# Key maxima of an agent-attention kernel: two scans of the scores in PSUM per chunk, one per half of the agents, in the place of one strided pass over the transposed scores

## The chip, the cores and the metric

The kernel runs on one core of a Trainium2 chip. The metric is the device time of one execution in microseconds (us). The time before is 364.25 us, the median of three runs (364.14, 364.25, 367.25).

## What is computed

Four batches of 12608 tokens with 128 channels, and 49 agents per batch. A softmax over all tokens (agents against keys) pools the values into 49 rows; a softmax over the agents (queries against agents) spreads these rows back over the tokens. Then a mixture-of-experts step replaces, per batch, the 128 tokens with the highest gate score.

```python
def sm(a, b):
    s = scale * (a @ b.transpose(0, 2, 1))
    s = s - s.max(-1, keepdims=True)
    e = np.exp(s)
    return e / (e.sum(-1, keepdims=True) + 1e-09)
a2k = sm(agents, k)          # (B, 49, 12608)
agent_v = a2k @ v
q2a = sm(q, agents)
x = q2a @ agent_v
...
top_idx = np.argpartition(-scores[b], capacity)[:capacity]   # scores = x @ w_gate
out[b, top_idx] = x[b, top_idx] + g[:, None] * ye            # ye: two-layer expert
```

The change touches one quantity of this: for each agent, the maximum of its scores over all keys, `s.max(-1)` in `a2k`.

## The kernel before, in words

**Tiling.** A batch's tokens are 99 columns of 128. They are worked in seven chunks (15, 15, 15, 15, 15, 15 and 9 columns). A chunk of keys or queries comes from memory with the channels on the partitions, 960 KB for 15 columns, into one of five input buffers (`inp`, shared with the values).

**Scores (`scores`, L205).** For each chunk, and for each half `h` of the agents (32 each, the 49 agents padded to 64), four matmuls write one PSUM tile `S`: matmul `i` puts 32 agents on partitions 32i to 32i+31, for a quarter of the chunk's tokens (480 columns for a 15-column chunk, 288 for a 9-column one). The four use different partitions of the tile. In a profile each of these fp32 matmuls leaves two records, so a half is 8 records and a chunk 16. VectorE then transposes the tile in blocks of 32x32 into an SBUF tile (`sk` for keys, `sq` for queries) in which tokens are on the partitions (L220). There are two `S` buffers in PSUM (SB = 2), one half each; a half is refilled when the instructions that read it are done.

**Key side.** `k_front` (L228) does the scores of a key chunk and then reduces the transposed tile to the chunk's maximum for each of 49 agents on each partition (L238, `mx`): the input is read as "p t a -> p a t", so that consecutive elements are 64 floats apart. After a batch's seventh chunk `k_max` (L242) takes the maximum over the chunks (L245, `m1`), turns it with a TensorE transpose (L247, `mT`), takes the maximum over the 128 partitions (L250, `m2`), spreads it over all partitions by a diagonal matrix (L252, `dg`) and a matmul with ones (L254, `mB`), and copies it to SBUF (L257, `mb`). `k_exp` (L264, L267) waits for `mb`: GpSimd subtracts it from each chunk, ScalarE takes the exponential. Then the matmuls `av` (L282) pool the values, `v_finish` makes the weights `ws` (L320 to L324).

**Query side.** `q_scores` (L329) does the same transposes, then a maximum over the agents of each token (L340, `qm`, read contiguously); `q_exp`, `q_high` and `q_low` make fp16 pairs `f` on GpSimd and ScalarE; `q_turn` transposes them on TensorE (`fT`, L392) and copies them out (`ft`, L393). `q_gate` (L407, `pg`) gives the gate scores, `topk` finds the 128 largest by 16 rounds of counting (L489 to L500, `jk`, `bk`, `js`), `q_out` (L448, `po`) makes the output tiles `og`, which are stored. `expert` gathers the chosen rows (L633), and scatters the new rows (L686) when the batch's output is stored.

**What sets the order.** The program is written chunk by chunk in the order of `load_order`, with priorities for some steps (RANK, TOPK, CHASE and so on). A scheduler then fixes one static order per engine, by its own model of durations; at run time each engine goes through its list in that order and waits where an operand isn't ready. So another duration or another number of instructions on one engine changes the lists of the others too.

Of the kernel before, what the change touches and what calls it, by code (L numbers as in the profile page):

```python
# [13 lines left out]
F32 = mybir.dt.float32  # L14
# [5 lines left out]
ALU = mybir.AluOpType  # L20
AX = mybir.AxisListType
PSUM = bass.MemoryType.PSUM

P = 128
# [3 lines left out]
A = 49  # L28
AP_ = 64
CHUNKS = [15, 15, 15, 15, 15, 15, 9]  # L30
STARTS = [sum(CHUNKS[:i]) for i in range(len(CHUNKS))]
NCH = len(CHUNKS)
# [93 lines left out]
def agent_attention_moe(ctx, tc, qT, kT, va, agT, wgb, w1, w2, consts, qs, outs, capacity):  # L126
    nc = tc.nc
# [13 lines left out]
    sm = ctx.enter_context(tc.tile_pool(name="sm", bufs=2))  # L141
# [39 lines left out]
    idf = const.tile([P, P], F32, name="idf")  # L181
# [3 lines left out]
    ones_f = const.tile([2 * A, P], F32, name="ones_f")  # L185
# [14 lines left out]
    def load(src, name, w):  # L200
        t = inp.tile([P, TMAX * (C + 1)], F32, tag="in", name=name)
        newest["load"] = nc.sync.dma_start(t[:, :w], src).ins
        return t

    def scores(src, b, c, dst):  # L205
        n = CHUNKS[c]
        w = 32 * n
        col = P * STARTS[c]
        xt = load(src[b, :, col:col + P * n], f"xT_{b}_{c}", P * n)
        for h in range(2):  # L210
            ps = psS.tile([P, 512], F32, tag="S", name=f"S_{b}_{c}_{h}")
            for i in range(4):
                nc.tensor.matmul(  # L213
                    ps[32 * i:32 * i + 32, :w],
                    ag_sb[:, b, 32 * h:32 * h + 32],
                    xt[:, w * i:w * i + w],
                    start=True,
                    stop=True,
                )
            nc.vector.transpose(  # L220
                dst[:, :n, 32 * h:32 * h + 32],
                ps[:, :w].rearrange("p (t c) -> p t c", c=32),
            )

    st = [{} for _ in range(B)]
    tail, begun, turns = set(), [], []
# [2 lines left out]
    def k_front(b, c):  # L229
        n = CHUNKS[c]  # L230
        d = st[b]
        if c == 0:
            d["S"] = {}
            d["mx"] = sm.tile([P, NCH, A], F32, tag="mx", name=f"mx_{b}")
        s = skp.tile([P, TMAX, AP_], F32, tag="sk", name=f"sk_{b}_{c}")
        scores(kT, b, c, s)
        d["S"][c] = s
        nc.vector.tensor_reduce(  # L238
            d["mx"][:, c], s[:, :n, :A].rearrange("p t a -> p a t"), axis=AX.X, op=ALU.max
        )  # L240

    def k_max(b):  # L242
        d = st[b]
        m1 = sm.tile([P, A], F32, tag="m1", name=f"m1_{b}", bufs=1)
        nc.vector.tensor_reduce(m1, d["mx"].rearrange("p c a -> p a c"), axis=AX.X, op=ALU.max)  # L245
        pt = psT.tile([P, 512], F32, tag="T", name=f"mT_{b}")
        nc.tensor.transpose(pt[:A, :P], m1, idf)  # L247
        yield
        m2 = sm.tile([A, 1], F32, tag="m2", name=f"m2_{b}", bufs=1)
        nc.vector.tensor_reduce(m2, pt[:A, :P], axis=AX.X, op=ALU.max)  # L250
        dg = sm.tile([P, A], F32, tag="m1", name=f"dg_{b}", bufs=1)[:A]
        nc.vector.tensor_scalar(dg, idf[:A, :A], m2, None, op0=ALU.mult)  # L252
        pb = psT.tile([P, 512], F32, tag="T", name=f"mB_{b}")
        nc.tensor.matmul(pb[:, :A], ones_f[:A], dg, start=True, stop=True)  # L254
        yield
        mb = sm.tile([P, A], F32, tag="mb", name=f"mb_{b}")
        nc.vector.tensor_copy(mb, pb[:, :A])  # L257
        d["mb"] = mb
        yield
# [72 lines left out]
    def q_scores(b, c):  # L332
        n = CHUNKS[c]
        d = st[b]
        s = qp.tile([P, TMAX, AP_], F32, tag="sq", name=f"sq_{b}_{c}", bufs=3)
        d["q", c] = s
        scores(qT, b, c, s)
        m = sm.tile([P, TMAX], F32, tag="qm", name=f"qm_{b}_{c}", bufs=3)
        d["qm", c] = m
        nc.vector.tensor_reduce(m[:, :n], s[:, :n, :A], axis=AX.X, op=ALU.max)  # L340
# [390 lines left out]
    for i in range(LAST):  # L731
# [15 lines left out]
        for b, c in get("k"):  # L747
            k_front(b, c)
            if c == NCH - 1:
                chains.append((b, k_max(b)))  # L750
# [105 lines left out]
```

## Time and profile before

| | |
|---|---|
| median of three runs | 364.25 us |
| the profiled execution | 367.46 us, of which its span from first to last instruction is 365.2 us |
| VectorE (DVE) busy | 287.6 us, 79% of the span, 761 instructions |
| TensorE (PE) busy | 308.0 us, 84% |
| GpSimd (POOL) busy | 182.9 us, 50% |
| ScalarE (ACT) busy | 169.6 us, 46% |
| chain that ended last | PE 52%, DVE 32%, POOL 5%, issue 4%, DMA 4%, ACT 2% |

The profiled execution lies 3.2 us above the median, near the slowest of the three runs. "Busy" is the time in which at least one instruction of an engine was under way. PEld is TensorE's loading of weights. The chain that ended last is followed back from the last instruction: at each step to what released it. In rows of waits, "A <- B: t, n" means that A's engine stood idle t us in n places until B was done. Lines of instructions are numbered as in the kernel before.

### The profile page before, as it was taken

How to read it: one execution, taken by the hardware profiler on the slowest of the kernel's cores; microseconds unless marked ns; L12 is line 12 of the kernel's file. 1: busy time of each engine (PE TensorE's matmuls, PEld its weight loads, DVE VectorE, ACT ScalarE, POOL GpSimd, SP SyncE). 2: the span in 40 equal slices, each digit the busy share in tenths (PEclk: the TensorE clock that was granted, in tenths of full speed). 3: DMA queues.
4: the chain of work that ended last, by engine and by line, in shares of the span. 5: the costliest groups of instructions: out<-in, count | busy, mean ns of one | idle time of the engine just before them, and what ended most of it. 6: DMA issues, size and time to landing. Idle time of an engine off the chain costs nothing.

```text
span 365.2 us, 9066 instructions
## 1 busy us (share of the span) xinstructions
PE 308.0 (84%) x3669; PEld 199.9 (55%) x3669; DVE 287.6 (79%) x761; ACT 169.6 (46%) x293; POOL 182.9 (50%) x149
## 2 busy tenths in 40 slices
PE   3775885998959999989999778989989999977774
PEld 0111344554435656446545438365479998967763
DVE  1999997669989998987899795176696989797432
ACT  1012455321544644645543156044667649796740
POOL 0046698714693655794415099033322015894532
PEclk9999997899987999999999995898999799996699
DMA  8999989689994999994998995455068875786390
GB/s 298 408 420 415 346 281 391 228 304 334 420 377 132 367 359 336 347 385 141 396 337 308 403 354 178 157 189 222 2 263 293 351 286 209 305 355 257 133 375 16
DMA packets 18586, 106.63 MB, mean 292 GB/s; under 512 B 2544, under 2 KB 3952, under 8 KB 18544
## 3 DMA queue, kind: packets, MB, share of 16 engines
q1 hardware_dynamic: 17472, 105.07, 75.5%
q8 instruction: 29, 0.48, 0.5%
q0 software_dynamic: 256, 0.52, 0.4%
q10 hardware_dynamic: 816, 0.46, 0.4%
q14 instruction: 13, 0.11, 0.1%
HBM read 79.83 MB, written 26.21 MB: 290 GB/s over the span
## 4 chain that ended last, share of the span: by engine, by line
PE 52%; DVE 32%; POOL 5%; issue 4%; DMA 4%; ACT 2%; POOLq 0%; ACTq 0%; DVEq 0%
PE S L213 17%; PE po L448 10%; PE av L282 9%; PE fT L392 6%; DVE mx L238 6%; DVE sk L220 5%; DVE sq L220 3%; PE pg L407 3%; DVE qm L340 2%; PE bk L494 2%; DMA cst<-consts 2%; DVE qm L351 2%; POOL sq L347 2%; DMA out<-og 1%; POOL f L373 1%
## 5 line engine op out<-in xcount | busy, mean ns | idle before, releaser
L213 PE MATMUL S<-xT,ag_sb 128*32 128x480 f32 (+1 forms) x896 | 117.0, 586 | 15.2 <-DMA ag_sb<-agT 6.3
L393 ACT COPY ft<-fT 98x896 f16<-98x896 f16 (+2 forms) x49 | 42.7, 899 | 58.4 <-PE fT L392 58.2
L448 PE MATMUL po<-ws,ft 98*128 98x128 f16 x792 | 63.7, 235 | 5.8 <-DVE ws L323 2.2
L347 POOL TENSOR_TENSOR sq<-sq,qm 128x735 f32<-128x735 f32 (+1 forms) x28 | 38.2, 1369 | 56.6 <-DVE qm L340 52.3
L448 PEld LDWEIGHTS <-ft 98*128 98x128 f16 x792 | 54.8, 107 | 14.2 <-issue 13.4
L282 PE MATMUL av<-v,sk 128*64 128x129 f32 x792 | 60.9, 291 | 0.6 <-ACT sk L267 0.6
L213 PEld LDWEIGHTS S<-xT,ag_sb 128*32 128x32 f32 x896 | 24.9, 113 | 61.5 <-issue 16.8
L282 PEld LDWEIGHTS av<-v,sk 128*64 128x64 f32 x792 | 50.2, 144 | 11.5 <-issue 7.5
L373 POOL TENSOR_TENSOR f<-sq,f 128x735 f16<-128x735 f32 (+1 forms) x28 | 41.2, 1476 | 28.7 <-ACT f L368 23.7
L264 POOL TENSOR_TENSOR sk<-sk,mb 128x735 f32<-128x735 f32 (+1 forms) x28 | 46.7, 1712 | 10.0 <-DVE mb L257 10.0
L220 DVE STREAM_TRANSPOSE sk<-S 128x480 f32<-128x480 f32 (+1 forms) x56 | 35.0, 640 | 12.0 <-PE S L213 11.2
L348 ACT ACTIVATE sq<-sq,lift 128x735 f32<-128x735 f32 (+1 forms) x28 | 24.8, 887 | 41.0 <-POOL sq L347 40.8
L392 PEld LDWEIGHTS <-f 128*98 128x98 f16 x396 | 26.9, 127 | 23.0 <-issue 16.4
L238 DVE TENSOR_REDUCE mx<-sk 128x49 f32<-128x735 f32 (+1 forms) x28 | 38.9, 1390 | 0.3
L392 PE MATMUL fT<-idh,f 128*98 128x128 f16 x396 | 34.1, 227 | 5.4 <-POOL f L373 4.5
L220 DVE STREAM_TRANSPOSE sq<-S 128x480 f32<-128x480 f32 (+1 forms) x56 | 34.7, 636 | 5.0 <-PE S L213 4.7
L368 ACT CAST f<-sq 128x735 f16<-128x735 f32 (+1 forms) x28 | 22.0, 789 | 31.2 <-POOL sq L362 24.5
L362 POOL TENSOR_TENSOR sq<-sq,qm 128x735 f32<-128x735 f32 (+1 forms) x14 | 19.1, 1367 | 31.7 <-DVE qm L355 28.2
L467 POOL TENSOR_TENSOR og<-og,r 128x512 f32<-128x512 f32 (+2 forms) x33 | 30.3, 946 | 7.6 <-ACT og L466 5.0
L496 DVE TENSOR_REDUCE bk<-bk 128x3 f32<-128x99 f32 x64 | 16.5, 259 | 21.1 <-PE bk L494 20.6
L457 ACT ACTIVATE og<-po,iv 128x512 f32<-128x512 f32 (+1 forms) x35 | 22.3, 669 | 20.6 <-PE po L448 13.4
L267 ACT ACTIVATE sk<-sk 128x735 f32<-128x735 f32 (+1 forms) x28 | 22.1, 797 | 18.7 <-POOL sk L264 18.2
(143 smaller groups left out, 380.4 us busy)
## 6 DMA issues: line engine op xcount, KB each, us to landing
v<-va SPq DMA_DIRECT2D x24, 967.5 KB, 6.9
xT<-kT SPq DMA_DIRECT2D x24, 960.0 KB, 7.9
xT<-qT SPq DMA_DIRECT2D x24, 960.0 KB, 8.3
out<-og SPq DMA_DIRECT2D x24, 960.0 KB, 4.3
v<-va SPq DMA_DIRECT2D x4, 580.5 KB, 4.8
xT<-kT SPq DMA_DIRECT2D x4, 576.0 KB, 6.5
xT<-qT SPq DMA_DIRECT2D x4, 576.0 KB, 5.6
out<-og SPq DMA_DIRECT2D x4, 576.0 KB, 5.9
```

What stands on the lines that cost most here:

```text
L213: nc.tensor.matmul(ps[32 * i:32 * i + 32, :w], ag_sb[:, b, 32 * h:32 * h + 32], xt[:, w * i:w * i + w], start=True, stop=True,)
L220: nc.vector.transpose(dst[:, :n, 32 * h:32 * h + 32], ps[:, :w].rearrange("p (t c) -> p t c", c=32),)
L238: nc.vector.tensor_reduce(d["mx"][:, c], s[:, :n, :A].rearrange("p t a -> p a t"), axis=AX.X, op=ALU.max)
L264: nc.gpsimd.tensor_tensor(sv, sv, st[b]["mb"].unsqueeze(1).broadcast_to([P, n, A]), op=ALU.subtract)
L282: nc.tensor.matmul(d["av"][o:o + AP_, :C + 1], d["S"][c][:, t], d["v", c][:, t], start=(j < 2), stop=(j >= COLS - 2),)
L347: nc.gpsimd.tensor_tensor(sv, sv, m[:, :n].unsqueeze(2).broadcast_to([P, n, A]), op=ALU.subtract)
L348: nc.scalar.activation(sv, sv, AF.Exp, scale=SCALE, bias=lift)
L373: nc.gpsimd.tensor_tensor(f[:, :n, A:], st[b]["q", c][:, :n, :A], f[:, :n, :A], op=ALU.subtract)
L392: nc.tensor.transpose(pt[:2 * A, P * t:P * t + P], f[:, t0 + t, :], idh)
L393: (nc.vector.tensor_copy if TURN[b][t0 // 8] == "V" else nc.scalar.copy)(d["ft", c][:2 * A, P * t0:P * (t0 + nt)], pt[:2 * A, :P * nt])
L448: nc.tensor.matmul(p3[:, t], q_tile(b, c, t0 + t), d["W"][:, i, :C], start=(i == 0), stop=(i == 1))
L467: nc.gpsimd.tensor_tensor(o4, o4, rate.broadcast_to([P, nt, C]), op=ALU.mult)
```

## The change

`scores` gets an argument `top`. On the key side, after each of the two transposes of a chunk, a VectorE reduction reads the same PSUM tile, contiguously along the tokens, and writes one maximum per partition (a partition being one agent of the half and one quarter of the tokens). The strided pass over `sk` goes. `mx` shrinks from 49 to 2 values per chunk and partition, and `k_max` works on 2 values per partition: the transpose gives 2 rows of 128, `m2` is the maximum over the four quarters, `dg` spreads it on a 2-row diagonal, and the matmul with ones has 2 rows and 64 columns.

```diff
-    def scores(src, b, c, dst):
+    def scores(src, b, c, dst, top=None):
...
                 ps[:, :w].rearrange("p (t c) -> p t c", c=32),
             )
+            if top is not None:
+                nc.vector.tensor_reduce(top[:, h:h + 1], ps[:, :w], axis=AX.X, op=ALU.max)
...
-            d["mx"] = sm.tile([P, NCH, A], F32, tag="mx", name=f"mx_{b}")
+            d["mx"] = sm.tile([P, NCH, 2], F32, tag="mx", name=f"mx_{b}")
...
-        scores(kT, b, c, s)
+        scores(kT, b, c, s, d["mx"][:, c])
         d["S"][c] = s
-        nc.vector.tensor_reduce(
-            d["mx"][:, c], s[:, :n, :A].rearrange("p t a -> p a t"), axis=AX.X, op=ALU.max
-        )
...
-        m1 = sm.tile([P, A], F32, tag="m1", name=f"m1_{b}", bufs=1)
-        nc.vector.tensor_reduce(m1, d["mx"].rearrange("p c a -> p a c"), axis=AX.X, op=ALU.max)
+        m1 = sm.tile([P, 2], F32, tag="m1", name=f"m1_{b}", bufs=1)
+        nc.vector.tensor_reduce(m1, d["mx"].rearrange("p c h -> p h c"), axis=AX.X, op=ALU.max)
         pt = psT.tile([P, 512], F32, tag="T", name=f"mT_{b}")
-        nc.tensor.transpose(pt[:A, :P], m1, idf)
+        nc.tensor.transpose(pt[:2, :P], m1, idf)
         yield
-        m2 = sm.tile([A, 1], F32, tag="m2", name=f"m2_{b}", bufs=1)
-        nc.vector.tensor_reduce(m2, pt[:A, :P], axis=AX.X, op=ALU.max)
-        dg = sm.tile([P, A], F32, tag="m1", name=f"dg_{b}", bufs=1)[:A]
-        nc.vector.tensor_scalar(dg, idf[:A, :A], m2, None, op0=ALU.mult)
+        m2 = sm.tile([2, 32], F32, tag="m2", name=f"m2_{b}", bufs=1)
+        nc.vector.tensor_reduce(
+            m2, pt[:2, :P].rearrange("h (i a) -> h a i", a=32), axis=AX.X, op=ALU.max
+        )
+        dg = sm.tile([2, 2, 32], F32, tag="dg", name=f"dg_{b}", bufs=1)
+        nc.vector.tensor_tensor(
+            dg, m2.unsqueeze(1).broadcast_to([2, 2, 32]),
+            idf[:2, :2].unsqueeze(2).broadcast_to([2, 2, 32]), op=ALU.mult,
+        )
         pb = psT.tile([P, 512], F32, tag="T", name=f"mB_{b}")
-        nc.tensor.matmul(pb[:, :A], ones_f[:A], dg, start=True, stop=True)
+        nc.tensor.matmul(pb[:, :AP_], ones_f[:2], dg.rearrange("k h a -> k (h a)"), start=True, stop=True)
```

The static order moves with it. Three places follow. In the names, `S_0_6_1` is batch 0, chunk 6, second half (`sk` and `sq` tell keys from queries); the last number is a counter. From L224 on, the changed kernel's lines are shifted by 2, and behind `k_max` by 4.

**VectorE at the end of batch 0's keys**, where `k_max` makes `mb`, before:

```order
L250 TENSOR_REDUCE m2_0_336<-mT_0_314 49x1
L340 TENSOR_REDUCE qm_0_3_357<-sq_0_3_342 128x15
L393 COPY ft_0_0_316<-fT_0_0_0_317 98x1024
L252 TENSOR_SCALAR dg_0_338<-idf_102,m2_0_336 49x49
L220 STREAM_TRANSPOSE sk_1_0_367<-S_1_0_0_370 128x15x32
L220 STREAM_TRANSPOSE sk_1_0_367<-S_1_0_1_376 128x15x32
L257 COPY mb_0_359<-mB_0_340 128x49
L238 TENSOR_REDUCE mx_1_366<-sk_1_0_367 128x49
```

and now:

```order
L249 TENSOR_REDUCE m2_0_343<-mT_0_321 2x32
L397 COPY ft_0_0_323<-fT_0_0_0_324 98x1024
L344 TENSOR_REDUCE qm_0_3_364<-sq_0_3_349 128x15
L253 TENSOR_TENSOR dg_0_345<-m2_0_343,idf_102 2x64
L220 STREAM_TRANSPOSE sk_1_0_374<-S_1_0_0_377 128x15x32
L225 TENSOR_REDUCE mx_1_373<-S_1_0_0_377 128x1
L220 STREAM_TRANSPOSE sk_1_0_374<-S_1_0_1_384 128x15x32
L225 TENSOR_REDUCE mx_1_373<-S_1_0_1_384 128x1
L261 COPY mb_0_366<-mB_0_347 128x49
```

Each transpose is followed by its scan. The copy of `mb_0` stood between the transposes and the pass of the next chunk; now it stands behind both transposes and both scans of it.

**TensorE at the scores of query chunk 3 of batch 3**, between the gate matmuls `pg` of batch 2, before:

```order
L407 MATMUL pg_2_2631<-ws_2_2551,ft_2_5_2478 128x3
L213 MATMUL S_3_3_0_2893<-xT_3_3_2891,ag_sb_94 32x480
L407 LDWEIGHTS ft_2_5_2478
L407 MATMUL pg_2_2631<-ws_2_2551,ft_2_5_2478 128x3
L213 MATMUL S_3_3_0_2893<-xT_3_3_2891,ag_sb_94 32x480
L407 LDWEIGHTS ft_2_5_2478
L407 MATMUL pg_2_2631<-ws_2_2551,ft_2_5_2478 128x3
L213 MATMUL S_3_3_0_2893<-xT_3_3_2891,ag_sb_94 32x480
```

and now:

```order
L411 MATMUL pg_2_2659<-ws_2_2579,ft_2_4_2390 128x3
L213 MATMUL S_3_3_0_2921<-xT_3_3_2919,ag_sb_94 32x480 x4
L213 MATMUL S_3_3_1_2927<-xT_3_3_2919,ag_sb_94 32x480 x3
L411 LDWEIGHTS ft_2_4_2390
L411 MATMUL pg_2_2659<-ws_2_2579,ft_2_4_2390 128x3
L213 MATMUL S_3_3_1_2927<-xT_3_3_2919,ag_sb_94 32x480
```

All eight score matmuls of the chunk stood alone, each between gate matmuls; now seven stand together and one alone. Key chunk 1 of batch 3 stood in the same way, in six pieces among `fT` matmuls; now its two halves are whole.

**TensorE at the scores of query chunk 0 of batch 2**, before:

```order
L213 MATMUL S_2_0_0_1472<-xT_2_0_1470,ag_sb_94 32x480 x4
L213 MATMUL S_2_0_1_1478<-xT_2_0_1470,ag_sb_94 32x480 x4
L448 LDWEIGHTS ft_0_6_730
L448 MATMUL po_0_6_4_2592<-ws_0_904,ft_0_6_730 128x128
L448 LDWEIGHTS ft_0_6_730
```

and now:

```order
L213 MATMUL S_2_0_0_1491<-xT_2_0_1489,ag_sb_94 32x480 x4
L286 MATMUL av_1_1150<-v_1_3_1507,sk_1_3_630 64x129 x15
L213 MATMUL S_2_0_1_1497<-xT_2_0_1489,ag_sb_94 32x480 x3
L498 LDWEIGHTS ones_b_111
L498 MATMUL bk_0_1067<-jk_hi_0_3_1123,ones_b_111 128x99
L498 LDWEIGHTS ones_b_111
L498 MATMUL bk_0_1067<-jk_hi_0_3_1123,ones_b_111 128x99
```

Here a half that was whole is now in two pieces (the fourth matmul follows behind the counting matmuls), and the second half stands behind 15 value matmuls. In the whole of TensorE's list the score halves were cut into pieces 12 more than the 112 halves (10 of 480 columns, 2 of 288); now they are cut into 9 more (6 and 3). SyncE's list, which issues the loads, has not changed.

## Rows read from the trace of the kernel before

**Rows 1.** [...] Under the dots the same view for line L238 alone: busy us of DVE and number of passes.
```profile
8.00:60.00 52.00, 38.13 (x376) 13.39 (x368) 48.68 (x76) 16.27 (x20) 30.89 (x21) 1.00 0.96 374
60.00:205.00 145.00, 132.40 (x1608) 75.68 (x1608) 128.84 (x289) 62.43 (x79) 82.64 (x58) 0.95 0.87 323
205.00:265.00 60.00, 53.34 (x562) 32.16 (x563) 38.18 (x103) 26.79 (x33) 27.76 (x18) 0.89 0.56 202
265.00:365.00 100.00, 82.42 (x1122) 78.13 (x1120) 71.14 (x289) 62.81 (x161) 40.73 (x43) 0.89 0.66 260
...
8.00:60.00 52.00, 14.28 (x10) 1.00 0.96 374
60.00:205.00 145.00, 24.64 (x18) 0.95 0.87 323
```

**Rows 2.** The chain that ended last in order of time: start us, length us, what. The first 40 us.
```profile
10.75 1.42 DVE mx L238
12.17 1.16 DVE sk L220 x2
13.36 1.48 DVE mx L238
14.83 1.16 DVE sk L220 x2
...
32.19 1.48 DVE mx L238
...
35.23 0.86 DVE mx L238
```

**Rows 3.** The waits of all engines from 8 to 60 us, and under the dots from 60 to 205 us: engine and line, for whom it waited, us in total, times, longest.
```profile
PEld S L213 <- DVE sk L220: 15.8, 19, 1.7
...
DVE sk L220 <- PE S L213: 4.7, 9, 0.9
PEld S L213 <- DVE sk L220: 0.8, 2, 0.5
```

**Rows 4.** Groups of instructions by line and shape: line, engine, operation, out<-in, shapes, count, then busy us and mean ns of one, then idle time before them.
```profile
L238 DVE TENSOR_REDUCE mx<-sk 128x49 f32<-128x735 f32 x24 | 35.2, 1468 | 0.2
L238 DVE TENSOR_REDUCE mx<-sk 128x49 f32<-128x441 f32 x4 | 3.7, 919 | 0.1
L340 DVE TENSOR_REDUCE qm<-sq 128x15 f32<-128x735 f32 x24 | 21.6, 902 | 0.2
L340 DVE TENSOR_REDUCE qm<-sq 128x9 f32<-128x441 f32 x4 | 2.4, 598 | 0.0
L220 DVE STREAM_TRANSPOSE sk<-S 128x480 f32<-128x480 f32 x48 | 31.4, 668 | 11.8 <-PE S L213 11.1
L220 DVE STREAM_TRANSPOSE sk<-S 128x288 f32<-128x288 f32 x8 | 3.7, 469 | 0.2 <-PE S L213 0.2
```

**Rows 5.** The same view for the small operations of `k_max`.
```profile
L245 DVE TENSOR_REDUCE m<-mx 128x49 f32<-128x343 f32 x4 | 3.1, 766 | 0.1
L252 DVE TENSOR_SCALAR dg<-idf,m 49x49 f32<-49x49 f32 x4 | 1.7, 434 | 0.0
L250 DVE TENSOR_REDUCE m<-mT 49x1 f32<-49x128 f32 x4 | 1.1, 263 | 0.6 <-PE mT L247 0.5
L257 DVE COPY mb<-mB 128x49 f32<-128x49 f32 x4 | 0.7, 166 | 0.0
```

**Rows 6.** The timeline around 42 us: start, length, engine, line, operation, out<-in, count, and in brackets the idle time before it.
```profile
41.91 0.16 DVE L257 COPY mb<-mB 128x49 f32<-128x49 f32 x1
...
42.15 1.80 POOL L264 TENSOR_TENSOR sk<-sk,mb 128x735 f32<-128x735 f32 x1 [1.37 <-DVE mb L257]
```

**Rows 7.** The chain again, at a whole chunk of scores, then in the two places where the score matmuls stood alone, and at a small one.
```profile
73.85 1.75 PE S L213 x16
...
160.00 0.92 PE S L213 x2
...
231.06 0.92 PE S L213 x2
...
238.32 0.92 PE S L213 x2
...
262.13 0.60 PE S L213 x2
```

**Rows 8.** The chain between 83 and 205 us, where it goes through the key maxima: the first and the last of nine such pieces, and the last of two maxima over the chunks.
```profile
83.59 1.44 DVE mx L238
...
203.87 0.91 DVE mx L238
204.81 0.78 DVE m L245
```

**Rows 9.** The timeline at the end: the gather of batch 2's rows, the transpose of them, and the scatter of its new rows.
```profile
335.19 0.99 POOL L633 DMA_INDIRECT xq<-q,idx  x1 [4.40 <-DVE js_lo L500]
...
345.21 0.42 PE L642 MATMUL qT<-idf,xq 128*128 128x128 f32 x1
...
359.77 1.03 POOL L686 DMA_INDIRECT out<-ye,idx  x1 [8.58 <-DVE ye L679]
```

**Rows 10.** Who let TensorE and its weight loads wait at the tiles `xT` (the loaded keys and queries), over the whole span: releaser, us, times.
```profile
  DVE sk L220: 21.1, 28
...
  DMA ag_sb<-agT: 12.6, 2
```

## The prediction

> **What bounds the kernel now.** I read the stages first (the windows view), because the key maxima lie in a part of the span only: 10 of the 28 strided passes run from 8 to 60 us, 18 from 60 to 205 us, none later [rows 1]. So 160 us of 365 can change only through an earlier start or another order. In the first stage VectorE is busy 48.68 of 52 us and TensorE 38.13; in the second TensorE leads, 132.40 of 145 us, with VectorE close behind at 128.84 [rows 1]. The chain in order of time shows the same for the start: it runs along VectorE, pass, two transposes, pass, two transposes, with nothing between [rows 2]. Then the waits: before 60 us TensorE's weight loads stood 15.8 us waiting for a transpose to free an `S` tile; after 60 us it was 0.8 us, and it was rather VectorE that waited for scores, 4.7 us [rows 3]. So in stage one a shorter VectorE list shortens the time; in stage two it can win at most what TensorE stands idle, 12.6 us (145 less 132.40), and no more than its part in that. Loads are no bound: the tiles `xT` made TensorE wait for transposes, and for a DMA only at the very start, for the agents [rows 10]. The DMA engines are 0.96 busy in stage one, though, so more than some 2 us (0.04 of 52) can't be won there unless loads already in their buffers give it.
>
> **Removed.** 24 passes of 1.468 us and 4 of 0.919: 38.9 us of VectorE [rows 4]. Per element the pass is slow: (1468 - 919) / (735 - 441) = 1.87 ns. The query maximum reads as many elements contiguously and takes (902 - 598) / 294 = 1.03 ns each, with 0.14 us fixed [rows 4].
>
> **Added.** 48 scans of 480 elements and 8 of 288. The trace has no such reduction from PSUM, so bounds: below, the maximum over 128 contiguous PSUM elements, 0.263 us [rows 5], with 352 more at 1.03 ns gives 0.626; above, the transpose, which reads the same tile and also writes all of it, 0.668 [rows 4]. It resembles the query maximum (0.14 + 480 x 1.03 ns = 0.64); I take 0.64, and 0.44 for 288 (0.43 to 0.469). Sum 48 x 0.64 + 8 x 0.44 = 34.2 us (33.5 to 35.8). By durations VectorE saves 4.7 us.
>
> One more thing helps: two transposes with no dependence between them take 1.16 us on the chain [rows 2], not 2 x 0.668, so neighbours overlap by some 0.09 us. The strided pass needed the transposes' results; a scan needs only the scores. A full chunk thus goes from 1.16 + 1.47 = 2.63 us to some 4 x 0.59 = 2.36, 0.27 us less, and a chunk of 9 columns changes by almost nothing. The 24 full chunks save 6.5 us; I take that.
>
> [...]
>
> **`k_max`.** `m1` goes from 343 strided elements (0.766 us) to 14: 0.17, as the small copy of `mb` (0.166) [rows 5]. `m2` reads 128 elements as before, but 32 apart: 0.26 to 0.38 (128 more or less at 1.03 or 1.87 ns, 0.14 fixed). `dg` goes from 0.434 to some 0.2. That is 0.8 us per batch, 3.2 in all. TensorE's transpose and matmul there keep their number. But the copy of `mb_0` now stands behind two scans of the next batch's first chunk: about 1.2 us later, which eats the 0.8. So for batch 0 I count nothing from `k_max`. What waits for `mb` is GpSimd's subtraction, which stood idle 1.37 us for it [rows 6] with `f` of a query chunk behind it; in the new list that `f` goes first, so this idle time is filled.
>
> **What it is worth, stage by stage.** (a) To 60 us: six full chunks of batch 0 save 6 x 0.27 = 1.6 us on the chain, the first chunks of batch 1 and the filled idle time a little more: 2 us (0 to 5). (b) 60 to 205 us: the chain passes nine key-maximum pieces, seven of full chunks, and two maxima over chunks [rows 8]: 7 x 0.27 + 2 x 0.6 = 3.1 us; I take 3 (0, if TensorE takes it all, to 6). (c) The order of the score matmuls. A whole chunk takes 1.75 us in 16 records, so 0.88 per half of four matmuls; one alone, between other matmuls, takes 0.92 us [rows 7]. Four that stand together on different partitions run at once; each piece that a half is cut into costs the same again. Before, the halves were cut into 10 more pieces of 480 columns and 2 of 288 (0.60 us, rows 7): 10.4 us; eight of the pieces lie between 231 and 239 us on the chain [rows 7]. Now 6 and 3: 7.3 us. That is 3.1 us less (0 to 5, as the new pieces fall on or off the chain). (d) The end. The transpose of batch 2's gathered rows, which ran at 345.21 us, opens its expert, whose scatter at 359.77 us still waited for it [rows 9]. In TensorE's list it stands three groups of output matmuls later than before, and GpSimd's gather, which itself waited for the counting (at 335.19 us, rows 9), three output multiplications later: 1.5 us longer (0 to 4). Sum: 2 + 3 + 3.1 - 1.5 = 6.6 us.
>
> The trace is of an execution of 367.46 us, 3.2 above the median; 367.46 - 6.6 = 360.9 for such a one. The runs to compare are medians, so I set the saving against 364.25: 357.6 us.
>
> **Longer hold, costed at nothing.** Each key tile `S` is now held for transpose and scan, 0.64 us longer per half. What covers it: with two tiles, a refill takes 0.88 us and VectorE works 1.2 us on the other half meanwhile; and after 60 us TensorE waited only 0.8 us for key tiles [rows 3]. If a query chunk follows a key chunk directly its second half comes some 0.4 us late; mostly a reduction of an older chunk stands between. Without this cover it is the third rival.
>
> **Rivals.** *All of it comes through:* (a) 5, (b) 6, (c) 3.1, no loss at the end: 14 us, 350 us. For it: VectorE is on the chain in both stages. Against: TensorE 91% busy in stage two [rows 1]. Chance 0.13.
> *Nothing comes through:* stage two is TensorE's, the new cuts of score halves fall on the chain where old ones were off it, the end grows by 4: 2 - 4 and a little of (b), 361 to 368 us, say 365. For it: 100 us at the end without any key work [rows 1]. Chance 0.26.
> *Slower, by the held tile:* after 60 us 18 key chunks have 36 halves, each held 0.64 us longer, 23 us in all. TensorE, busy 91%, pays where it comes back for a tile at once. If it pays half, 11.5 us eat the 6.6: 369 us. It decides from 10.3 us on (3.7 above today), 0.29 us per half. Against: the 0.8 us of today [rows 3]. Chance 0.11. [...]
> *The change doesn't do what it says:* a scan costs what the strided pass does per element, 0.14 + 480 x 1.87 ns = 1.04 us; 48 of these and 8 of 0.68 are 55 us, 16.5 more than the passes. With half of that on the chain, 372 us. Against: the transpose reads the tile at (668 - 469) / 192 = 1.04 ns per element [rows 4]. [...]
>
> **Numbers.** The forecast, 357.6 us, has the rest, 0.47, with its own range 354 to 361. A measurement of this kernel tells about 1% from no change: faster means below 360.6, slower above 367.9. Faster: 0.42 of the forecast and 0.13, 0.55. Same: 0.05 and 0.25 of the second rival, 0.30. Slower: 0.11, 0.03 and 0.01, 0.15. The range leaves out half of the first rival and the two slower ones: 350 to 367.5.
>
> **What would show it.** In the profile after: scans of 0.63 to 0.67 us, 56 of them, some 34 us, and VectorE's busy time some 8 to 10 us less; `m1` below 0.25 us. The first `mb` 1 to 2 us earlier. TensorE's waits for key tiles between 60 and 205 us not much above 1 us; several us there would be the held tile. One score half at a time near 160 and 231 us, and lone pieces of 0.92 us elsewhere. The last scatter later against the last output store than before. Falls of TensorE's granted clock at other places (0.95 and 0.89 in the later stages, rows 1) aren't priced and could move the time by some us either way; another order at the end could do the same.

## The result, and the profile after

The kernel after takes 354.75 us (median of 354.79, 355.55, 354.29 and 354.71), the kernel before 364.41 us (median of 364.14, 364.25, 364.58 and 367.25): ratio 0.972, 95% interval 0.967 to 0.977. Forecast were 357.6 us and a saving of 6.6; the saving is 9.7 us. The profiled execution of after took 354.79 us with a span of 353.0, that of before 367.46 with 365.2, so these two traces differ by 12 us, 2 to 3 more than the medians.

The windows view of after: one line per stretch, from and to in us, then its length, busy us (and number of instructions) of PE, PEld, DVE, ACT and POOL, the granted TensorE clock as a share of full speed, the busy share of the DMA engines and GB/s. The first three stretches are those of [rows 1], the last ends with the span.

```profile
8.00:60.00 52.00, 39.90 (x387) 13.63 (x379) 48.49 (x89) 16.71 (x20) 32.41 (x22) 1.00 0.97 385
60.00:205.00 145.00, 134.54 (x1629) 75.55 (x1632) 123.31 (x308) 63.94 (x80) 81.18 (x58) 0.94 0.87 325
205.00:265.00 60.00, 55.78 (x833) 40.87 (x826) 48.07 (x157) 37.84 (x52) 32.21 (x22) 1.00 0.73 272
265.00:353.00 88.00, 71.15 (x821) 66.11 (x818) 56.15 (x232) 49.93 (x143) 36.73 (x40) 0.83 0.59 237
```

VectorE is as busy as before to 60 us and 5.5 us less from 60 to 205 us. From 205 to 265 us, where no key maximum is left to take, TensorE gets 833 matmuls done instead of 562, at a granted clock of 1.00 instead of 0.89. Over the span VectorE is busy 276.8 us, 10.8 less than before.

The groups of VectorE by line and shape in after (as rows 4 and 5):

```profile
L225 DVE TENSOR_REDUCE mx<-S 128x1 f32<-128x480 f32 x48 | 29.7, 619 | 0.0
L225 DVE TENSOR_REDUCE mx<-S 128x1 f32<-128x288 f32 x8 | 3.4, 421 | 0.0
L244 DVE TENSOR_REDUCE m<-mx 128x2 f32<-128x14 f32 x4 | 0.6, 144 | 0.0
L249 DVE TENSOR_REDUCE m<-mT 2x32 f32<-2x128 f32 x4 | 1.0, 258 | 0.5 <-PE mT L246 0.5
L253 DVE TENSOR_TENSOR dg<-m,idf 2x64 f32<-2x64 f32 x4 | 1.1, 279 | 0.1
```

The scans take 33.1 us in all, beside the 38.9 us of the passes. The waits of after, from 8 to 60 us and under the dots from 60 to 205 us (as rows 3):

```profile
PEld S L213 <- PE S L213: 13.4, 11, 1.8
PEld S L213 <- issue: 9.0, 10, 2.0
PE S L213 <- DVE mx L225: 3.3, 6, 1.1
...
DVE sk L220 <- PE S L213: 7.4, 7, 1.7
...
PE S L213 <- DVE mx L225: 1.7, 2, 1.3
```

The key tile is now freed by a scan, where it was freed by a transpose. After 60 us TensorE's matmuls wait 1.7 us for two scans: the held tile is no several-us wait there. But VectorE waits longer for key scores, 7.4 us against 4.7.

To see where the time came from I cut both traces at five events: the copy of the last maximum `mb_3`, the first matmul of the query chunk `S_3_3`, the last matmul of `av_3`, the last output matmul `po`, and the end of the last expert's `ye`.

| us | mb_3 | S_3_3 starts | av_3 ends | last po ends | last ye ends |
|---|---|---|---|---|---|
| before | 209.5 | 231.0 | 261.3 | 349.6 | 361.3 |
| after | 204.7 | 222.0 | 244.6 | 332.6 | 349.0 |
| difference, by stretch | -4.8 | -4.2 | -7.7 | -0.3 | +4.7 |

The first three stretches gain, the fourth hardly changes and the last gives back. The chain of after where before cut the chunk `S_3_3` into eight pieces [rows 7], and a chunk after it:

```profile
222.04 1.74 PE S L213 x14
223.78 0.11 PE pg L411
223.89 0.92 PE S L213 x2
...
238.37 1.75 PE S L213 x16
```

One piece is cut off now, and it costs 0.92 us, as a lone piece did before. And the end, in the timelines of after and then of before:

```profile
263.60 0.15 DVE L583 CAST idx<-ji 128x1 uint32<-128x1 f32 x1
...
323.08 0.15 DVE L583 CAST idx<-ji 128x1 uint32<-128x1 f32 x1
...
330.54 0.39 PE L646 MATMUL qT<-idf,xq 128*128 128x128 f32 x2
...
347.53 1.03 POOL L690 DMA_INDIRECT out<-ye,idx  x1 [12.90 <-DVE ye L683]
```

```profile
275.65 0.15 DVE L579 CAST idx<-ji 128x1 uint32<-128x1 f32 x1
...
334.76 0.15 DVE L579 CAST idx<-ji 128x1 uint32<-128x1 f32 x1
```

The first two rows of each are the indices of batch 1 and of batch 2. They lie 59.5 and 59.1 us apart, since batch 2 is counted behind batch 1, round by round; and from batch 2's indices to its scatter it is 24.4 us here and 25.0 before [rows 9]. So in these two traces the end of the kernel follows the counting of batch 1, and that came 12 us earlier, while the output groups came 17 us earlier. The difference is near the 4.7 us. (The distance of the two indices isn't fixed: in the other runs of after's order below it is 55.6 to 59.0 us.) Behind the transpose `qT` of the gathered rows after is slower than before: 17.0 us to the scatter instead of 14.6, with TensorE at half clock (a granted clock of 0.5) in 6.8 us of it instead of 1.1.

### The profile page after: what moved, and what is told of

The parts are those of the page before. It is cut to its first block, busy times and chain, and to the rows that moved or that the text cites. A ratio compares the mean times of both kernels' runs of the same rounds, so it can differ in the third digit from the quotient of the medians.

```text
span 353.0 us, 9115 instructions
## 1 busy us (share of the span) xinstructions
PE 303.3 (86%) x3669; PEld 196.8 (56%) x3669; DVE 276.8 (78%) x789; ACT 169.7 (48%) x293; POOL 183.4 (52%) x149
## 4 chain that ended last, share of the span: by engine, by line
PE 57%; DVE 26%; issue 6%; POOL 5%; DMA 3%; ACT 2%; POOLq 0%; ACTq 0%; DVEq 0%
PE S L213 18%; PE po L452 12%; PE av L286 11%; PE fT L396 6%; DVE sk L220 3%; PE pg L411 3%; DVE mx L225 3%; DVE sq L220 3%; DMA cst<-consts 2%; PE bk L498 2%; POOL sk L268 2%; DVE qm L344 2%; DVE qm L355 1%; PE ph L668 1%; DVE rank L553 1%
## 5 line engine op out<-in xcount | busy, mean ns | idle before, releaser
L213 PE MATMUL S<-xT,ag_sb 128*32 128x480 f32 (+1 forms) x896 | 113.4, 580 | 19.7 <-DMA ag_sb<-agT 6.1
L213 PEld LDWEIGHTS S<-xT,ag_sb 128*32 128x32 f32 x896 | 23.6, 111 | 66.3 <-issue 29.9
L286 PE MATMUL av<-v,sk 128*64 128x129 f32 x792 | 57.9, 282 | 0.1
L286 PEld LDWEIGHTS av<-v,sk 128*64 128x64 f32 x792 | 47.7, 139 | 11.8 <-issue 7.2
L377 POOL TENSOR_TENSOR f<-sq,f 128x735 f16<-128x735 f32 (+1 forms) x28 | 41.1, 1472 | 22.0 <-ACT f L372 18.5
L220 DVE STREAM_TRANSPOSE sk<-S 128x480 f32<-128x480 f32 (+1 forms) x56 | 36.0, 642 | 13.9 <-PE S L213 13.8
L396 PEld LDWEIGHTS <-f 128*98 128x98 f16 x396 | 26.0, 124 | 20.8 <-issue 14.9
L396 PE MATMUL fT<-idh,f 128*98 128x128 f16 x396 | 33.3, 224 | 2.8 <-POOL f L377 2.5
L225 DVE TENSOR_REDUCE mx<-S 128x1 f32<-128x480 f32 (+1 forms) x56 | 33.1, 590 | 0.0
L461 ACT ACTIVATE og<-po,iv 128x512 f32<-128x512 f32 (+1 forms) x35 | 22.6, 669 | 21.2 <-PE po L452 20.5
L372 ACT CAST f<-sq 128x735 f16<-128x735 f32 (+1 forms) x28 | 22.0, 790 | 18.5 <-POOL sq L366 12.8
L344 DVE TENSOR_REDUCE qm<-sq 128x15 f32<-128x735 f32 (+1 forms) x28 | 24.1, 862 | 0.1
```

The lines of the kernel that those rows point to most:

```text
L213: nc.tensor.matmul(ps[32 * i:32 * i + 32, :w], ag_sb[:, b, 32 * h:32 * h + 32], xt[:, w * i:w * i + w], start=True, stop=True,)
L220: nc.vector.transpose(dst[:, :n, 32 * h:32 * h + 32], ps[:, :w].rearrange("p (t c) -> p t c", c=32),)
L225: nc.vector.tensor_reduce(top[:, h:h + 1], ps[:, :w], axis=AX.X, op=ALU.max)
L286: nc.tensor.matmul(d["av"][o:o + AP_, :C + 1], d["S"][c][:, t], d["v", c][:, t], start=(j < 2), stop=(j >= COLS - 2),)
L377: nc.gpsimd.tensor_tensor(f[:, :n, A:], st[b]["q", c][:, :n, :A], f[:, :n, :A], op=ALU.subtract)
L396: nc.tensor.transpose(pt[:2 * A, P * t:P * t + P], f[:, t0 + t, :], idh)
```

## The experiments

Three theories are set against each other; the first two are reasons for the gain. **Theory A:** VectorE's shorter work. **Theory B:** the other static order that came with it (score halves whole around 231 us, no stretch at half clock from 220 to 250 us). **Theory C**, beside them, is the held tile as a cost inside the gain. Ratios are to the runs of before on the same chip, whose medians were 366.62 us (first four runs), 364.82 us (next four) and 368.44 us (last four).

**Shorter passes, order of before.**

```diff
-            d["mx"][:, c], s[:, :n, :A].rearrange("p t a -> p a t"), axis=AX.X, op=ALU.max
+            d["mx"][:, c], s.rearrange("p t a -> p (t a)")[:, :A * n].rearrange("p (a t) -> p a t", t=n), axis=AX.X, op=ALU.max
```

> The kernel before, with its pass over the transposed scores reading as many elements (735 or 441) lying one behind the other, into a result of the same shape. The slots then hold maxima over other elements, still one number per agent for all partitions, so the softmax is shifted by other constants. Every engine's order is the one of before, row for row; only the pass is shorter: at the scan's slope ((619 - 421) ns / 192 elements = 1.03 ns) 0.88 us and 0.58 us instead of 1.468 and 0.919, so VectorE does 24 x 0.59 + 4 x 0.34 = 15 us less. Theory A (shorter work of VectorE is what pays): more of it is saved than the change saved (10.8 us), so 352 to 359 us, and the eight-piece chunk S_3_3 at 231 us shrinks with it. Theory B (the other order pays: score halves left whole, no stretch at half clock from 220 to 250 us): 361 to 366 us, S_3_3 still takes about 8 us.

Measured: 361.49 us, 0.987 [0.978, 0.995]. Its pass, by line and shape:

```profile
L238 DVE TENSOR_REDUCE mx<-sk 128x49 f32<-128x735 f32 x24 | 21.8, 910 | 0.2
```

The stride alone made the pass slow: 910 ns instead of 1468 for as many elements. VectorE is busy 277.0 us, to 0.2 us what the change leaves it, and about half the gain is there (0.5 to 2.2% by the interval, of 2.8%). The time and `S_3_3`, which stays at 8.25 us, are as theory B put them; but before took 366.62 us here, and against that the shorter passes alone do bring something, less than theory A asks. Neither theory holds by itself.

**The scan on the transposed scores in SBUF, contiguous, then strided; and the PSUM scan strided.** The same line of after, three ways:

```diff
-                nc.vector.tensor_reduce(top[:, h:h + 1], ps[:, :w], axis=AX.X, op=ALU.max)
+                nc.vector.tensor_reduce(top[:, h:h + 1], dst[:, :n, 32 * h:32 * h + 32], axis=AX.XY, op=ALU.max)
...
+                nc.vector.tensor_reduce(top[:, h:h + 1], dst[:, :n, 32 * h:32 * h + 32].rearrange("p t a -> p a t"), axis=AX.XY, op=ALU.max)
...
+                nc.vector.tensor_reduce(top[:, h:h + 1], ps[:, :w].rearrange("p (t c) -> p c t", c=32), axis=AX.XY, op=ALU.max)
```

> The kernel after, with the scan reading the half's transposed scores in SBUF (480 or 288 elements in runs of 32) and not the PSUM tile, which so comes free at the end of the transpose again. The maxima are then over groups of slots, one number per agent for all partitions. The order differs from both kernels. Theory A: VectorE does as much work as after (scan 0.55 to 0.70 us), so 350 to 358 us; if holding the PSUM tile costs the first 34 us their gain, the first batch's key transposes end 2 to 5 us before 34.3. Theory B: anything from 352 to 366, as the order falls.

> As the run with the scan on the transposed scores in SBUF, but read with a stride (slot by slot, 256 bytes from element to element, as the pass of before read them). Every engine's order is that run's, row for row. At the pass's 1.468 us / 735 = 2.0 ns per element the scan takes 0.96 us (480) and 0.58 us (288): VectorE does 48 x 0.34 + 8 x 0.16 = 18 us more in the same order. Theory A: slower than that run by 5 to 15 us. Theory B: within 2 us of it.

> The kernel after, with the scan of the PSUM tile reading the same 480 or 288 elements with a stride of 128 bytes. Order row for row that of after. If a stride in PSUM costs what the pass's stride in SBUF cost (2.0 ns per element), the scans take 0.96 and 0.58 us and VectorE does 18 us more: Theory A then says 360 to 370 us, theory B 354 to 357. If the scan stays at 0.62 us, a stride costs nothing in PSUM, the time stays 354 to 356 by both theories, and the run tells only that.

Measured: 344.23 us, 0.935 [0.925, 0.945]; 357.46 us, 0.969 [0.958, 0.979]; 355.41 us, 0.972 [0.962, 0.982]. The scans of the three, by line and shape:

```profile
L225 DVE TENSOR_REDUCE mx<-sk 128x1 f32<-128x480 f32 x48 | 30.6, 640 | 0.7
```

```profile
L225 DVE TENSOR_REDUCE mx<-sk 128x1 f32<-128x480 f32 x48 | 47.9, 1001 | 0.7
```

```profile
L225 DVE TENSOR_REDUCE mx<-S 128x1 f32<-128x480 f32 x48 | 29.7, 618 | 0.0
```

The first is faster than either theory allowed (350 to 358, 352 to 366): how much of that is its order and how much the tile that comes free early is measured below. Its last key transpose of batch 0 ends at 32.4 us, 1.9 before after's. Between the first two, order row for row the same, VectorE's busy time differs by 16.7 us (275.6 and 292.3) and the ratio by 0.034, some 12 us: there most of its work is on the path, as theory A has it. The third tells of the chip alone: a stride of 128 bytes costs nothing in PSUM (618 ns, and 619 without it in after), and the time is that of after.

**Work and order apart.** All instructions of TensorE, VectorE, ScalarE and GpSimd are tied, each to the one ahead of it, in the order that another kernel has (issue order only, no new wait). The edit is one call and its function; `ORDER` is the table of places.

```diff
     while side or late:
         step()
+    in_order(tc)
...
+def in_order(tc):
+    traced = tc.nc.cur_bb.bb.instructions
+    how = mybir.DependencyInfo(mybir.DependencyClass.NoSync, mybir.DependencyReason.DATA)
+    for engine, packed in ORDER.items():
+        mine = [i for i in traced if i.engine == getattr(mybir.EngineType, engine)]
+        steps = np.frombuffer(zlib.decompress(base64.b85decode(packed)), np.int16)
+        row = [mine[j] for j in np.cumsum(steps.astype(int))]
+        for a, b in zip(row, row[1:]):
+            tc.add_manual_dep(b, a.name, how, reason="order")
```

> The kernel after, with every instruction of TensorE, VectorE, ScalarE and GpSimd kept in the order of the kernel before; each scan stands directly behind its transpose, where before the pass stood behind both. VectorE does 10.8 us less than before, as in the run with the contiguous pass, whose order is the same and which took 0.987 of before. Theory A (shorter work alone): the gain of the change is there, 353 to 357 us, ratio near 0.972. Theory B (shorter work is half, the new order the other half): 0.983 to 0.992, so about 360 to 363 us. Theory C (holding the PSUM tile over the scan costs several us, which the new order makes up for): 0.99 to 1.01, slower than the run with the contiguous pass.

> The kernel before, with every instruction of the four engines in the order of the kernel after; the strided pass of a chunk stands where its second scan stood. VectorE does what it did before. Theory A: the order alone gives nothing, 0.995 to 1.01. Theory B: it gives its half, 0.98 to 0.99, about 359 to 363 us. If the order of after was right only for its shorter work: over 1.01.

Measured: after's work in before's order 364.17 us, 0.996 [0.993, 1.000] (10 runs); before's work in after's order 365.42 us, 1.000 [0.996, 1.005] (10 runs). So:

| ratio to before | order of before | order of after |
|---|---|---|
| work of before | 1 | 1.000 |
| work of after | 0.996 | 0.972 |

Neither part alone brings 1%; together they bring 2.8%. The contiguous pass, with nearly the same work and no held tile, brought 1.3% in before's order; the intervals of that run and of 0.996 overlap by 0.002. Theories A and B both fall as they were put: A fits the order alone (0.995 to 1.01) but not the work alone, B neither. The work alone lies in theory C's range (0.99 to 1.01), slower than the contiguous pass. In before's order the held tile may thus eat part of what the shorter work wins; no run has the SBUF scan in that order, so how much stays open. Shown is that the change's work and its order pay as a pair. Where each part goes is seen in the five events (us; in brackets the stretch before the event):

| | mb_3 | S_3_3 starts | av_3 ends | last po ends | last ye ends |
|---|---|---|---|---|---|
| before's work, after's order | 210.7 | 232.7 (22.0) | 255.3 (22.6) | 342.0 (86.7) | 360.6 (18.6) |
| after's work, before's order | 208.0 | 227.3 (19.3) | 257.6 (30.3) | 342.7 (85.1) | 354.4 (11.7) |
| contiguous pass, before's order | 206.3 | 225.3 (19.0) | 254.0 (28.7) | 341.7 (87.7) | 355.0 (13.3) |

Stretches can be compared here, whole rows less so: the traced run of the second row took 360.22 us, the shortest of its ten (median 364.17), and the trace of before 367.46. The stretch from `S_3_3` to `av_3` goes by the order, 28.7 to 30.3 us or 22.6, whatever VectorE's work (in the 28.7 no half clock falls, in each 30.3 there are 3.4 us of it). The last stretch does too: 11.7 to 13.3 us in before's order, 16.4 and 18.6 in after's. By the order alone 7.7 us are won in the one and 6.9 lost in the other. And the first stretch goes by both: shorter work moves `mb_3` by 6.0 us in after's order, in before's by 1.5, and by 3.2 with the contiguous pass.

The windows of the last stretch, of before's work in after's order, of before, and of after:

```profile
342.00:345.00 3.00, 0.35 (x2) 0.12 (x1) 0.88 (x5) 1.59 (x8) 2.04 (x3) 0.98 0.79 328
345.00:352.00 7.00, 6.42 (x28) 6.00 (x28) 1.13 (x7) 0.30 (x2) 0.00 (x0) 0.52 0.39 154
352.00:360.60 8.60, 6.70 (x41) 6.24 (x40) 3.23 (x6) 0.00 (x0) 1.03 (x1) 0.80 0.01 2
```

```profile
349.60:361.30 11.70, 8.77 (x70) 7.89 (x68) 4.70 (x14) 1.48 (x7) 2.62 (x3) 1.00 0.49 200
```

```profile
332.60:349.00 16.40, 11.25 (x70) 10.06 (x69) 5.24 (x18) 1.87 (x10) 3.06 (x4) 0.79 0.30 121
```

The same 70 to 71 matmuls. In after's order batch 2's indices come only 9 to 10 us before the last output matmul ends (14 to 16 in before's), so the short exchanges that open its expert run after the output is done, when TensorE is busy 0.35 of 3 us; then the clock falls, and the expert's matmuls run at a granted clock of 0.52, about half. Over all fourteen traces this stretch goes with the half clock in it: 11.7 to 11.8 us with 0.2 us of it or none, 13.2 to 13.3 with 3.4, 16.4 with 6.8 (after), 18.5 to 18.7 with 10.2. The five traces of after's order, one of them with whole halves, have the 6.8 and the 10.2.

**The held tile apart.** The same function, with the PSUM scan and the SBUF scan in each other's order.

> The run with the scan on the transposed scores in SBUF (344 us in its own order), with the order of the kernel after on the four engines. The scan's place is unchanged and its duration nearly so (640 for 619 ns); the PSUM tile comes free at the transpose's end. Theory C (the held tile costs): 343 to 349 us. Theory B (that run's gain over after is its order): 352 to 356 us, as after.

> The kernel after (scan of the PSUM tile), with the order of the run whose scan reads SBUF. Theory C: the held tile takes that run's gain away again, 351 to 358 us. Theory B (the order): 343 to 347 us, as that run.

Measured: 354.28 us, 0.973 [0.966, 0.980], and 350.32 us, 0.959 [0.950, 0.969]. In after's order it makes no difference when the tile comes free (0.973 and 0.972); the first is tied to its order and after isn't, so the tying costs nothing to be seen either. In the SBUF scan's own order holding the tile takes 0.024 away, and what is left of that run's lead over after, 0.013, is its order (the intervals of 0.959 and 0.972 overlap by 0.002); 350.32 us lies between the ranges of the two theories (351 to 358, 343 to 347), just under theory C's. Theory C holds there in the main and not in after's order. The windows of the first stage of that order, tile freed early and then held:

```profile
8.00:60.00 52.00, 39.93 (x391) 14.61 (x387) 50.01 (x92) 17.30 (x21) 33.15 (x22) 0.98 0.99 393
```

```profile
8.00:60.00 52.00, 36.99 (x342) 11.95 (x334) 44.83 (x85) 16.09 (x20) 31.06 (x21) 0.97 0.89 342
```

With the tile held VectorE loses 5.2 us of work in 52, and even the loads fall back (0.99 to 0.89). `mb_3` then comes at 203.8 us instead of 198.0.

**Halves made whole.** The same function; in the table the four matmuls of each cut half now stand together where the first stood, in before's order, in after's, and in that of a third version, which is the run with the SBUF scan, but with one maximum for each half of the agents (by itself that is the third run below):

```diff
-        m2 = sm.tile([2, 32], F32, tag="m2", name=f"m2_{b}", bufs=1)
-        nc.vector.tensor_reduce(
-            m2, pt[:2, :P].rearrange("h (i a) -> h a i", a=32), axis=AX.X, op=ALU.max
-        )
...
+        m2 = sm.tile([2, 1], F32, tag="m2", name=f"m2_{b}", bufs=1)
+        nc.vector.tensor_reduce(m2, pt[:2, :P], axis=AX.X, op=ALU.max)
...
+            dg, idf[:2, :2].unsqueeze(2).broadcast_to([2, 2, 32]), m2, None, op0=ALU.mult
```

> The kernel before, every engine's order kept but for five halves of key or query scores whose four matmuls stood apart (12 pieces more than halves): each now stands whole where its first matmul stood. If the apart matmuls cost TensorE time on the path (0.87 us each, 10.4 us in all, as the prediction's third term counts): 354 to 359 us, ratio 0.972 to 0.985, the chunk S_3_3 in about 2 us instead of 8.25, and the stretch from its start to the end of av_3 about 6 us shorter than 30.3. If TensorE waits there for something else anyway: 0.995 to 1.005, and what the chunk gains is lost before av_3 ends.

> The kernel after, its eight cut halves made whole in the same way (9 pieces more than halves). If apart matmuls cost time on the path: 9 x 0.87 = 7.8 us less, 346 to 350 us, ratio 0.95 to 0.96. If not: 353 to 356 us, ratio near 0.972.

> The run with the scan on the transposed scores in SBUF, with one maximum for each half of the agents (over all tokens and agents of the half), subtracted from every score of that half. Each engine's order is that run's. As that run: 342 to 347 us, ratio 0.93 to 0.945. A version to keep, faster than both kernels.

> The version with one maximum for each half, its eight cut halves of scores made whole (13 pieces more than halves). If apart matmuls cost time on the path: 13 x 0.87 = 11 us less, 332 to 338 us. If not: 342 to 347 us.

Measured: 362.80 us, 0.987 [0.981, 0.994]; 352.77 us, 0.957 [0.950, 0.964]; 347.06 us, 0.945 [0.939, 0.951]; and 341.95 us (335.99 to 343.11; the runs spread too far for an interval), 0.928 of before's median. The chain of the first at the two halves of `S_3_3`:

```profile
229.32 0.94 PE S L213 x8
230.26 0.22 PE pg L407 x5
230.48 0.94 PE S L213 x8
```

The chunk takes 2.17 us instead of 8.25, and the stretch from there to the end of `av_3` is 22.7 us instead of 30.3 (28.7 in the trace without half clock there): the whole halves are what after's order wins there, but for some 1.6 us that go with the clock. But over the kernel 12 pieces bring 5.6 us (368.44 to 362.80), not 10.4, between the two ranges that were set: from `av_3` to the last `po` it is 92.4 us instead of 88.3, with TensorE at half clock in 37 us of it against 20. In after 9 pieces bring 0.972 to 0.957, about 5.5 us of 7.8 (by the two intervals 2 to 9 us), in the ratio that was set for pieces on the path. What 13 bring in the last version stays open with that spread: its median lies just under the range for no gain (342 to 347). The versions with one maximum for each half beat both kernels.

## Why the prediction was right

The direction and the range were right, the saving 3 us too small.

**The durations held.** Scans 619 and 421 ns (0.64 and 0.44 taken), 33.1 us in all (34.2); `m1` 144 ns (0.17), `m2` 258 (0.26 to 0.38), `dg` 279 (some 0.2); VectorE 10.8 us less (8 to 10). The rival of a scan at the strided price (1.04 us for 480 elements, chance 0.03) is out. That price is the stride's alone: the pass takes 1.468 us with it and 0.910 contiguous, in the run with the contiguous pass.

**(a) To 60 us: 2 us counted, 1.1 came.** `mb_0` is copied at 40.79 us instead of 41.91 (1 to 2 us were named), but the last transpose of batch 0's keys ends at 34.3 us, before it at 34.4. VectorE stayed as busy. The hold isn't the reason that it was less than counted: in after's order with the tile freed at the transpose (the SBUF scan in after's order) that transpose ends at 34.4 us and `mb_0` comes at 40.72. Which wait took the rest stays open. That the hold costs nothing came out for this order; in the SBUF scan's own order `mb_0` comes at 43.19 us with the tile held and at 40.05 without.

**(b) 60 to 205 us: 3 us counted, 3.7 came** (4.8 at `mb_3` less the 1.1). TensorE's waits for key tiles stayed small, 1.7 us against 0.8, as named. That this saving needs the new order was not foreseen: in the old order after's work moves `mb_3` by 1.5 us.

**(c) Order of the score matmuls: 3.1 us counted, 7.7 came between `S_3_3` and `av_3`.** The place and the price of a piece (0.92 us) were right. Mis-sized was the term itself: it set 12 old pieces against 9 new ones, but eight old ones stood on the chain in one place and only one new piece stands there. That chunk went from 8.25 to 2.85 us, 5.4 of the 7.7; some 1.6 more go with 3.4 us of half clock that before had behind it and after hadn't. And a price per piece doesn't add up over the kernel: 12 pieces at 0.87 us brought 5.6 us.

**(d) The end: 1.5 us of loss counted, 4.7 came.** The place was right, the reason only in part. The transpose of the gathered rows comes 2.1 us before the last output matmul ends, instead of 4.4: 2.3 us, not far from what was counted. But it runs 7.5 us behind the indices instead of 10.4; late are the indices themselves, which moved by 12 us when the output moved by 17. The counting of two batches, one behind the other, was not followed to its start. The other 2.4 us lie behind the transpose (17.0 us to the scatter instead of 14.6), where the granted clock fell 1.5 us after the last output matmul and stayed at half for 6.8 us; the prediction had named such falls and not priced them.

**Not priced: 4.2 us between `mb_3` and `S_3_3`.** Before spent 10.2 us of this stretch at half clock, after none; the windows of before and of after:

```profile
209.50:231.00 21.50, 17.62 (x227) 13.10 (x225) 15.96 (x44) 10.92 (x14) 18.87 (x12) 0.76 0.72 255
```

```profile
204.70:222.00 17.30, 14.12 (x229) 10.13 (x228) 14.03 (x41) 11.08 (x15) 17.02 (x11) 1.00 0.93 374
```

As many matmuls keep TensorE busy 3.5 us longer. In the runs of after's order the stretch takes 17.3 us without half clock (also with the SBUF scan in it), 18.7 with 3.4 us of it (whole halves), 19.8 with 6.8 and 22.0 with 10.2, so it goes with the clock, by some 0.46 us per us of half clock (an estimate from the first and the last). The prediction's last sentence on the trace left this open. Over the whole span the clock differs little: 49.6 us at half clock before, 46.2 after, worth some 1.6 us at that price. So the clock isn't what the change won: what after gains by it here it loses again at the end.

The sum -1.1 - 3.7 - 4.2 - 7.7 - 0.3 + 4.7 is -12.3 us, that of these two traces. That the forecast came within 3 us is in part luck: (c) was 4.6 us too small, (d) 3.2 us too small a loss, and the two errors pull opposite ways. The sum also adds what the work wins and what the order wins as if each came by itself; by themselves they bring 0.4% and nothing. What stays open is which neighbours in the order make the shorter work pay: the table of work and order shows that it is the pair, not which rows of it.

## What to carry to other kernels

In a statically ordered kernel a shorter instruction changes the order as well, and the two have to be tried apart: here each of the two alone was worth under 1%, together 2.8%. Follow the chain that ends last back to where it starts: what another stretch wins is lost if that chain (here the counting of one batch behind another) does not start earlier too. With before's work in after's order the scores of `S_3_3` won 7.7 us, batch 1's indices came only 1.3 us earlier, and 6.9 us were lost at the end. And before moving a reduction to another place, read it contiguously where the result allows: the same pass with its stride taken out gave about half the gain in an unchanged order. (Its maxima are over other elements, which the softmax here allows, since any one number per agent can be subtracted.)

## What the runs showed of the hardware

A stride of 256 bytes costs VectorE 0.36 us in SBUF (640 to 1001 ns for 480 elements), one of 128 bytes nothing in PSUM (619 and 618 ns); no run has the same stride in both. Matmuls on different partitions ran at once only where they stood together: the four of a half take 0.94 us above (in 8 records), and one cut off takes 0.92 us by itself (in 2). And what an order wins on TensorE can be lost in part to the clock: with whole halves in before's order the mean granted clock was 0.903 to 0.907 in all four runs, with the cut ones 0.923 to 0.932 in the seven beside them. Why it fell more often there is not shown.
